# Retention followed by a token-mixing MLP: contiguous q, 128x128 state products, a last batch by chunks, and a new order

## Chip, cores and metric

The kernel runs on one core of a Trainium2 chip. A core has a tensor engine (PE, with its weight loads listed as PEld), a vector engine (DVE), a scalar engine (ACT), GpSimd (POOL), a sync engine (SP) that issues the transfers here, and 16 DMA engines. The metric is the time of one launch in microseconds (us); lower is better.

## The reference

Two blocks follow each other. The first is retention over q, k, v of shape (4 batches, 8 heads, 768 steps, 64), as a recurrence with a decay per head:

```python
gamma = 1.0 - 2.0 ** (-5.0 - np.arange(H))
for t in range(S):
    state = gamma * state + einsum('bhd,bhe->bhde', k[:, :, t], v[:, :, t])
    y[:, :, t] = scale * einsum('bhd,bhde->bhe', q[:, :, t], state)
```

Its output, with the heads side by side, is x of shape (4, 768, 512). The second block mixes tokens within a batch:

```python
W_tok = scale * einsum('bsd,btd->bst', x @ w_q, x @ w_k)
mixed = einsum('bst,btd->bsd', W_tok, x)
out = np.maximum(mixed, 0.0) @ w_out
```

w_q and w_k are 512x64, w_out is 512x512. Inputs and output are float32; the kernel multiplies in bfloat16 and accumulates in float32.

## The kernel before

**Tiles.** A batch has 768 steps: six chunks of 128, taken as three pairs of chunks. There are 12 pairs, numbered 0 to 11, three to a batch; pairs 9 to 11 are the last batch. The eight heads are four head pairs (`HP = 4`), two heads of 64 columns side by side (`x` = 0, 1). In the steps' names the first number is the pair and the second a chunk or a half.

**Retention by chunks.** For a pair the kernel casts k to bfloat16 (`ck`), multiplies v by a decay factor per step and head (`cv`) and casts q (`cq`). PE transposes k and q (`trk`, `trq`), and `ek`, `eq` copy the results from PSUM to SBUF. `sc` multiplies k and q into scores, `eat` applies the causal mask, `ia` multiplies the masked scores with the values, `st` adds the chunk's k and v product to the running state in PSUM bank 7, `es` copies the state to SBUF, and `in` (with `ic` for one type) multiplies q with the carried state. `ex` takes the sum from PSUM, times a decay factor, to x.

**The MLP.** `xt` transposes x on PE, `exT` copies it, `wqk` makes the w_k product (rows are steps) and the w_q product (rows are features), `ew` copies both. The mixing has no mask, so it is factored: `zm` accumulates z, the product of the w_k part and x, over a batch; `ez` copies z; `mx` multiplies z with the w_q part; `r` is the relu; `pj` multiplies by w_out, 4 matmuls of 512 columns to a chunk; `eo` copies the chunk to an output tile; and SP stores it.

**How q lies.** q is loaded with eight steps in a row to a partition, so after the transposes it is in order of (chunk, step, sub-position). `eq` copies it into `qT[128, 2, J*QG, HP]`, and the score matmuls read their moving operand as

```python
return pairs[p]["qT"][rows(x), c, :, hp]
```

that is, with a step of four elements. The products with the carried state read the same slice as their stationary operand.

**Three types of pairs.** `TYPES = "112112111nnn"` says how a pair's k and v are loaded. Types 1 and 2 bring two steps of one head together, runs of 512 bytes; type 1 then splits chunk from chunk in its casts, two instructions on 64 partitions for one chunk, and type 2 keeps the steps interleaved and does its scores and state products in 64x64 tiles. Type n loads one step to a partition, runs of 256 bytes, and casts a chunk in one instruction on 128 partitions.

**Tile forms on PE.** Scores, carried-state products and mixes contract over 64 rows, with the two heads or halves on the two row tiles of the array. State products and z have 64 output rows and use two column tiles. Transposes, values, w products and projections use the whole array.

**Order.** Nothing is scheduled by a compiler. `ORDER` is a list of steps written out by hand; each engine executes its own steps in the order of the list and waits on semaphores. A token `name.pair.part:E@bank` gives the engine (A for ACT, V for DVE, P for GpSimd, none for PE) and the PSUM bank. `fill.15@6` at the start is 15 matmuls on zeros. `LOADS` is the order in which SP issues transfers; a load is issued when one of 16 stage tiles (`STAGES`) is free, that is, when the load 16 places earlier has been cast. The stores (`s0` and so on) stand behind all loads.

Of the kernel before, what the change touches and what calls it, by code (L numbers as in the profile page):

```python
# [16 lines left out]
mask.0:P mask.1:P mask.2:P fill.15@6 ck.0.1:A cv.0.0:P cq.0.1:V cq.0.0:A trq.0@0 ck.1.0:P ck.0.0:V  # L17
eq.0:A cv.0.1:V cv.1.0:P trk.0@6 cv.1.1:P cv.3.1:P st.0.0 cv.3.0:P es.0.0:V ek.0:A sc.0.1@5
eat.0.1:V ck.3.1:P cv.2.1:P sc.0.0@0 in.0.1@2 ck.1.1:A cq.1.0:V trk.1@4 cq.1.1:A eat.0.0:V st.0.1
ek.1:A trq.1@6 eq.1:V sc.1.0@5 cq.2.1:A cq.2.0:V es.0.1:A sc.1.1@0 eat.1.0:V trq.2@4 ia.0.0@2 ck.2:A  # L20
ia.0.1@2 ex.0:V W:P st.1.0 eq.2:A ia.1.0@5 ck.4.1:P cq.4.0:P ck.4.0:P trk.2@4 cv.4.1:P es.1.0:A
st.1.1 in.1.1@5 cv.4.0:P cq.3.0:A eat.1.1:V cq.5:P es.1.1:A in.1.0@5 ek.2:A cq.3.1:V ck.3.0:A WO.0:P
xt.0@2 ia.1.1@5 ck.5.0:P ck.7.0:P trq.3@0 cv.5.0:P ex.1:V ck.6.0:P sc.2.1@3 eq.3:A cq.7:P eat.2.1:V
sc.2.0@5 trk.3@3 xt.1@0 ek.3:A cv.2.0:V st.2.0 eat.2.0:V es.2.0:V ck.6.1:P cv.6.1:P sc.3.1@3
eat.3.1:V in.2@5 exT.0:A exT.1:A ic.2@5 ia.2.0@5 ia.2.1@5 ex.2:V cq.4.1:A sc.3.0@1 st.3.0 es.3.0:A
wqk.0@3 trq.4@0 eat.3.0:V xt.2@6 ew.0:A eq.4:A trk.4@5 ia.3.1@3 in.3.1@3 exT.2:V ia.3.0@3 ex.3:V
cq.6.0:P st.3.1 cv.6.0:P wqk.1@6 ek.4:A wqk.2@5 ew.2:A sc.4.1@2 sc.4.0@0 ew.1:A cv.7.1:P ck.5.1:V
xt.3@4 exT.3:A zm.2@5 es.3.1:V zm.0@5 cq.8.0:P eat.4.1:V zm.1@5 st.4.0 eat.4.0:V ia.4.1@2 ck.8.1:P
trq.5@4 eq.5:V ez.0:A mx.0@5 es.4.0:A in.4.0@2 mx.2@0 in.4.1@2 r.0:A st.4.1 es.4.1:A WO.1:V ia.4.0@2
cq.9:P trk.5@4 ek.5:A wqk.3@6 ew.3:A pj.0.0@5 eo.0.0:A ex.4:V xt.4@2 sc.5.0@3 sc.5.1@5 r.2:A  # L30
cv.8.0:P cv.5.1:V st.5.0 es.5.0:A ck.7.1:A exT.4:V pj.0.1@2 eat.5.0:V eat.5.1:V cv.8.1:P wqk.4@0
ew.4:A ic.5@3 in.5@3 ia.5.0@3 eo.0.1:V ia.5.1@3 ck.9.1:P cv.9.1:P ex.5:V mx.1@0 r.1:A cq.6.1:A
ck.10.0:P trk.7@6 trq.7@2 cv.9.0:P ek.7:V trk.6@5 xt.5@3 exT.5:V pj.1.0@4 eo.1.0:A trq.6@6 eq.6:A
wqk.5@3 ew.5:A ek.6:V cq.10:P pj.2.0@4 eo.2.0:A eq.7:V sc.7.1@5 sc.6.0@1 st.6.0 es.6.0:A zm.3@3
ck.11.0:P zm.5@3 zm.4@3 ez.1:A st.6.1 es.6.1:A cv.7.0:V ck.10.1:P pj.2.1@4 eo.2.1:A st.7.0 eat.6.0:V
sc.7.0@2 eat.7.1:V es.7.0:A mx.5@0 sc.6.1@5 r.5:A pj.1.1@4 eo.1.1:A eat.7.0:V cq.8.1:A eat.6.1:V
cq.11:P ia.7.1@2 ia.7.0@2 st.7.1 in.7.0@2 in.7.1@2 ex.7:V mx.3@0 in.6.1@4 es.7.1:V pj.5.0@6 ia.6.1@4
r.3:A eo.5.0:A ia.6.0@4 trq.8@0 trq.9@6 ex.6:V pj.3.0@1 ck.8.0:A trk.8@5 xt.7@4 eq.8:V cv.10.0:P
eq.9:A ek.8:A eo.3.0:V pj.5.1@6 eo.5.1:A ck.9.0:V mx.4@0 r.4:A exT.7:V cv.10.1:P sc.8.1@2 eat.8.1:V
sc.8.0@4 eat.8.0:V st.8.0 es.8.0:A pj.3.1@6 eo.3.1:A trk.9@0 ek.9:V pj.4.1@2 eo.4.1:A xt.6@4 exT.6:V  # L40
# [27 lines left out]
def kernel(  # L68
# [9 lines left out]
):  # L78

# [49 lines left out]
    z_left = [NP] * B  # L129
# [13 lines left out]
    def load(name, p, half=None, eng=None):  # L143
# [11 lines left out]
        if TYPES[p] == "n":  # L155
            st[name + "_st"] = stage_pool.tile([128, 2, HP, 2, D], FP32, name=name + "_st", tag="st")
            for c in range(2):
# [34 lines left out]
    def load_token(token):  # L192
        if token[0] in "wo":
            load_weights(token)
        else:
            load(token[0], int(token[1:]))
# [8 lines left out]
    def more_loads():  # L205
        while queue:
            token = queue[0]
            if token[0] == "s":
                if not stored(token[1:]):
                    return  # L210
                queue.pop(0)
                continue
            n = len(staged)
            if n >= STAGES and staged[n - STAGES] not in cast:
                return
            staged.append(token)
            load_token(queue.pop(0))
# [15 lines left out]
    make_identity(nc, identity)  # L233

# [208 lines left out]
    def trk(e, b, p):  # L443
        st = pairs[p]
        ps = bank16(b).rearrange("p (hp i n) -> p hp i n", hp=HP, i=2)
        for hp in range(HP):
            for i in range(2):
                src = st["ks"][:, hp, i] if TYPES[p] == "2" else st["ks"][:, i, hp]
                nc.tensor.transpose(ps[:, hp, i], src.rearrange("p x d -> p (x d)"), identity)  # L449
        st["kT_ps"] = bank16(b)  # L450

    def ek(e, b, p):
        st = pairs[p]
        st["kT"] = kq_pool.tile([128, HP, 2, 128], BF16, name="kT")
        copy(e, st["kT"].rearrange("p hp i n -> p (hp i n)"), st["kT_ps"])
# [13 lines left out]
    def trq(e, b, p):  # L469
        st = pairs[p]  # L470
        ps = bank16(b).rearrange("p (c j n) -> p c j n", c=2, j=J)
        for j in range(J):
            nc.tensor.transpose(  # L473
                ps[:, :, j], st["qs"][:, j].rearrange("p x d -> p (x d)"), identity
            )
        st["qT_ps"] = bank16(b)

    def eq(e, b, p):
        st = pairs[p]
        st["qT"] = kq_pool.tile([128, 2, J * QG, HP], BF16, name="qT")  # L480
        copy(e, st["qT"].rearrange("p c t w -> p (c t w)"), st["qT_ps"])

    def qT(p, x, hp, c):
        return pairs[p]["qT"][rows(x), c, :, hp]
# [48 lines left out]
    state_ps = bank32(7)[:, 0 : HP * D].rearrange("p (hp d) -> p hp d", hp=HP)  # L533
# [13 lines left out]
    def inter(e, b, p, c):  # L547
        y = y_of(p, b)
        s_sb = pairs[p]["s", 0] if c == 1 else pairs[p - 1]["s", 1]
        for hp in range(HP):  # L550
            for x in range(2):
# [3 lines left out]
                    rhs=s_sb[rows(x), hp, :],  # L555
# [15 lines left out]
    def inter2(e, b, p):  # L571
        y = y_of2(p, b)
        for hp in range(HP):
            for c in range(2):
                s_sb = carried(p, c)
                if s_sb is None:
# [4 lines left out]
                    rhs=s_sb[rows(c), hp, :],  # L581
# [5 lines left out]
    def cross2(e, b, p):  # L587
        y = y_of2(p, b)
        new = [first(p, 0) if p % NP else False, first(p, 1)]
        for hp in range(HP):  # L590
            for i in range(2):
                for c in range(2):
                    x = 1 - c
                    s_sb = carried(p, c)
                    if s_sb is None:
# [4 lines left out]
                        rhs=s_sb[rows(x), hp, :],  # L600
# [5 lines left out]
    def state1(e, b, p, c):  # L606
        cp = p % NP
        st = pairs[p]
        for hp in range(HP):
            for x in range(2):  # L610
                nc.tensor.matmul(  # L611
                    out=state_ps[rows(x), hp, :],
# [7 lines left out]
    def state2(e, b, p, c):  # L620
        cp = p % NP
        st = pairs[p]
        for hp in range(HP):
            for j in range(2):
                for x in range(2):
                    nc.tensor.matmul(
                        out=state_ps[rows(x), hp, :],
# [7 lines left out]
    def es(e, b, p, c):  # L635
        pairs[p]["s", c] = s_pool.tile([128, HP, D], BF16, name="s_sb")
        copy(e, pairs[p]["s", c], state_ps)

    def ia1(e, b, p, half):
        st = pairs[p]  # L640
        y = y_of(p, b)
        for hi in range(2):
            hp = 2 * half + hi
            for c in range(2):
                for x in range(2):
# [7 lines left out]
                    )  # L653

# [32 lines left out]
    def ex(e, b, p):  # L687
        st = pairs[p]
        st["x"] = x_pool.tile([128, 2, HP, 2, D], BF16, name="x_nat")
        nc.vector.tensor_tensor(  # L690
            out=st["x"].rearrange("p c hp x d -> p x (c hp) d"),
            in0=st["y_ps"].rearrange("p x c hp d -> p x (c hp) d"),
            in1=fy[:, p % NP].rearrange("p x c hp -> p x (c hp)").to_broadcast([128, 2, 2 * HP, D]),
            op=ALU.mult,
        )

    def xt(e, b, p):
        st = pairs[p]
        ps = bank16(b).rearrange("p (a c t) -> p a c t", a=NDM, c=2)
        for c in range(2):  # L700
            for a in range(NDM):
                nc.tensor.transpose(  # L702
                    ps[:, a, c], st["x"][:, c, a].rearrange("p x d -> p (x d)"), identity
                )
        st["xt_ps"] = bank16(b)

    def exT(e, b, p):
        st = pairs[p]
        st["xT"] = xt_pool.tile([128, NDM, 2, C], BF16, name="xT")
        copy(e, st["xT"].rearrange("p a c t -> p (a c t)"), st["xt_ps"])  # L710

    def wqk(e, b, p):
        st = pairs[p]
        wk_ps = bank32(b)[:, 0:128].rearrange("p (h0 c h1) -> p c h0 h1", h0=J, c=2)
        wq_ps = bank32(b)[:, 128:384]
        for c in range(2):
            for a in range(NDM):
                nc.tensor.matmul(  # L718
                    out=wk_ps[:, c, :],
                    lhsT=st["xT"][:, a, c, :],  # L720
                    rhs=wqk_sb[:, a, 2 * DH :],
                    start=(c == 0 and a == 0),
# [166 lines left out]
```

## Time and profile before

| | us |
|---|---|
| Time, median of 3 runs | 103.09 (102.55 to 103.23) |
| Profiled execution, its own time | 102.75 |
| Its span, first to last instruction | 101.0 |
| PE busy | 90.5 |
| DVE busy | 75.4 |
| ACT busy | 63.7 |
| GpSimd busy | 63.2 |
| Bytes moved | 26.69 MB, a mean of 264 GB/s |

The granted clock is TensorE's clock as a share of full speed; its mean over the span is 0.949. A line such as `PE banks L494 x16` in the chain is a run of 16 matmuls at line 494 of the kernel (here a score step); the time beside it is what the chain spent there. A group's line gives busy time and the mean of one instruction in ns, then the idle time ahead of it and what ended it. Matmuls overlap, so the mean of one (288 ns for a score) is far more than its share of the array; the chain's time over a run of them is the cost to use.

### The profile page before, as it was taken

The numbers are of one execution on the slowest core, as the hardware profiler recorded it, in microseconds if no ns is written. First come the engines' busy times: TensorE is split into PE (matmuls) and PEld (weight loads), VectorE is DVE, ScalarE is ACT, GpSimd is POOL, SyncE is SP. The second block draws the span as 40 slices with busy tenths as digits, with TensorE's granted clock in tenths as the row PEclk, the third lists the DMA queues.
The fourth block names the chain that finished last, engine by engine and source line by source line (L and its number), as shares of the span: only waits on it lengthen the run. The fifth ranks groups of instructions, "written<-read, shape, count | busy, mean of one in ns | idle before, by whom it ended". The sixth has DMA issues, their size and how long they took to land.

```text
span 101.0 us, 3421 instructions
## 1 busy us (share of the span) xinstructions
PE 90.5 (90%) x1439; PEld 64.5 (64%) x1439; DVE 75.4 (75%) x107; ACT 63.7 (63%) x101; POOL 63.2 (62%) x87
## 2 busy tenths in 40 slices
PE   5994296996889999999999999999999999999950
PEld 1323186894779889669776776678977777553410
DVE  4217497599996798998899889979687964749510
ACT  4357649488778467975757798664686665623540
POOL 7853999999999998899999999996100000000000
PEclk9999555589999999999999999999999999999999
DMA  0999999998999999999998999999935000522983
GB/s 28 335 276 336 322 353 373 349 305 187 357 341 277 372 352 366 375 380 361 351 243 204 232 299 230 290 292 394 402 116 208 6 0 0 214 108 100 379 313 139
DMA packets 39407, 26.69 MB, mean 264 GB/s; under 512 B 14304, under 2 KB 32736, under 8 KB 39392
## 3 DMA queue, kind: packets, MB, share of 16 engines
q1 hardware_dynamic: 38864, 26.22, 83.6%
q10 hardware_dynamic: 528, 0.26, 0.9%
q8 instruction: 11, 0.18, 0.8%
q14 instruction: 4, 0.03, 0.1%
HBM read 20.19 MB, written 6.29 MB: 262 GB/s over the span
## 4 chain that ended last, share of the span: by engine, by line
PE 71%; DVE 7%; DMA 7%; issue 4%; ACT 3%; POOL 3%; SPq 1%; DVEq 0%; POOLq 0%
PE banks L798 19%; PE banks L494 10%; DMA v_st<-in_v_dram 7%; PE banks L646 5%; PE banks L727 5%; PE banks L449 5%; PE banks L473 5%; PE banks L702 4%; PE banks L611 4%; POOL vs L412 3%; PE banks L718 3%; PE banks L756 3%; PE banks L776 2%; PE banks L552 2%; DVE qT L135 2%
## 5 line engine op out<-in xcount | busy, mean ns | idle before, releaser
L412 POOL TENSOR_TENSOR vs<-v_st,fv 64x512 bf16<-64x512 f32 x24 | 26.4, 1099 | 3.8 <-DMA v_st<-in_v_dram 2.4
L798 PE MATMUL banks<-wout_sb,relu 128*128 128x512 bf16 x96 | 23.9, 380 | 0.0
L526 DVE TENSOR_TENSOR at_sb<-banks,cmask 128x1024 bf16<-128x1024 f32 x18 | 21.5, 1219 | 1.1 <-PE banks L494 0.8
L134 ACT COPY o_st<-banks 128x512 f32<-128x512 f32 x19 | 11.1, 586 | 12.0 <-PE banks L798 11.7
L690 DVE TENSOR_TENSOR x_nat<-banks,fy 128x1024 bf16<-128x1024 f32 x10 | 12.2, 1220 | 4.5 <-PE banks L646 3.1
L798 PEld LDWEIGHTS <-relu 128*128 128x128 bf16 x96 | 8.3, 98 | 8.5 <-issue 0.9
L135 POOL CAST ks<-k_st 64x512 bf16<-64x512 f32 (+1 forms) x21 | 12.9, 621 | 1.0 <-PE banks L449 0.2
L494 PE MATMUL banks<-qT,kT 64*128 64x128 bf16 x160 | 12.0, 288 | 1.2 <-DVE qT L135 0.8
L791 ACT ACTIVATE relu<-banks 128x1024 bf16<-128x1024 f32 x9 | 9.2, 1027 | 2.9 <-PE banks L776 2.9
L134 ACT COPY kT<-banks 128x1024 bf16<-128x1024 bf16 x8 | 8.1, 1014 | 3.5 <-PE banks L449 3.5
L494 PEld LDWEIGHTS <-kT 64*128 64x128 bf16 x160 | 7.9, 107 | 2.8 <-issue 1.9
L611 PE MATMUL banks<-vs,ks 128*64 128x64 bf16 x144 | 5.9, 208 | 3.1 <-POOL vs L412 3.1
L134 ACT CAST ks<-k_st 64x512 bf16<-64x512 f32 (+2 forms) x12 | 7.8, 654 | 1.2 <-DMA k_st<-in_k_dram 1.1
L449 PE MATMUL banks<-identity,ks 128*128 128x128 bf16 x96 | 7.9, 230 | 0.7 <-DVE at_sb L526 0.7
L134 ACT COPY qT<-banks 128x1024 bf16<-128x1024 bf16 x7 | 7.1, 1013 | 2.2 <-PE banks L473 2.2
L473 PE MATMUL banks<-identity,qs 128*128 128x128 bf16 x96 | 8.1, 234 | 0.3 <-ACT qs L134 0.3
L135 POOL CAST qs<-q_st 128x1024 bf16<-128x1024 f32 (+1 forms) x8 | 7.7, 962 | 0.7 <-DMA q_st<-in_q_dram 0.4
L646 PE MATMUL banks<-vs,at_sb 128*128 128x64 bf16 x160 | 8.0, 201 | 0.0
L526 DVE TENSOR_TENSOR at_sb<-banks,cmask_n 128x1024 bf16<-128x1024 f32 x6 | 7.2, 1219 | 0.9 <-PE banks L494 0.7
L134 ACT CAST s_sb<-banks 128x256 bf16<-128x256 f32 x16 | 6.0, 375 | 2.9 <-PE banks L611 1.7
L611 PEld LDWEIGHTS <-ks 128*64 128x64 bf16 x144 | 4.2, 117 | 5.6 <-issue 4.6
L727 PE MATMUL banks<-xT,wqk_w 128*128 128x256 bf16 x48 | 7.2, 273 | 0.3 <-issue 0.3
(80 smaller groups left out, 156.7 us busy)
## 6 DMA issues: line engine op xcount, KB each, us to landing
q_st<-in_q_dram SPq DMA_DIRECT2D x12, 512.0 KB, 6.8
v_st<-in_v_dram SPq DMA_DIRECT2D x9, 512.0 KB, 7.0
out_dram<-o_st SPq DMA_DIRECT2D x9, 512.0 KB, 6.3
k_st<-in_k_dram SPq DMA_DIRECT2D x8, 512.0 KB, 6.9
k_st<-in_k_dram SPq DMA_DIRECT2D x7, 256.0 KB, 4.2
v_st<-in_v_dram SPq DMA_DIRECT2D x6, 256.0 KB, 5.4
out_dram<-o_st SPq DMA_DIRECT2D x6, 256.0 KB, 2.0
o_st<-in_moe_w_out_dram SPq DMA_DIRECT2D x2, 512.0 KB, 6.1
```

What stands on the lines that cost most here:

```text
L134: return nc.scalar.copy(out=out, in_=in_)
L135: return ENGINES[e].tensor_copy(out=out, in_=in_)
L412: ENGINES[e].tensor_tensor(out=st["vs"][rows(j), c].rearrange("p hp x d -> p (hp x) d"), in0=st["v_st"][rows(c), :, :, j].rearrange("p hp ...
L449: nc.tensor.transpose(ps[:, hp, i], src.rearrange("p x d -> p (x d)"), identity)
L473: nc.tensor.transpose(ps[:, :, j], st["qs"][:, j].rearrange("p x d -> p (x d)"), identity)
L494: nc.tensor.matmul(out=ps[:, x, hi, c, :], lhsT=st["kT"][rows(x), hp, c, :], rhs=qT(p, x, hp, c), start=(hi == 0 and c == 0), stop=(hi == ...
L526: ENGINES[e].tensor_tensor(out=st["at", half].rearrange("p x hi i t -> p (x hi i t)").rearrange("p (m n) -> p m n", n=n), in0=st["at_ps", ...
L611: nc.tensor.matmul(out=state_ps[rows(x), hp, :], lhsT=st["ks"][:, c, hp, x, :], rhs=st["vs"][:, c, hp, x, :], start=(cp == 0 and c == 0 an ...
L646: nc.tensor.matmul(out=y[:, x, c, hp, :], lhsT=st["at", half][:, x, hi, c, :], rhs=st["vs"][:, c, hp, x, :], start=first(p, x), stop=False ...
L690: nc.vector.tensor_tensor(out=st["x"].rearrange("p c hp x d -> p x (c hp) d"), in0=st["y_ps"].rearrange("p x c hp d -> p x (c hp) d"), in1 ...
L727: nc.tensor.matmul(out=wq_ps, lhsT=wqk_sb[:, a, 0 : 2 * DH], rhs=st["xT"][:, a].rearrange("p c t -> p (c t)"), start=False, stop=(a == NDM ...
L798: nc.tensor.matmul(out=bank32(b), lhsT=st["relu"][:, a, c, :], rhs=wout_sb[:, a, :], start=(a == 0), stop=(a == NDM - 1),)
```

## The change

- **q.** The transposes of q multiply by `identity_q`, the identity with its columns regrouped, so that a head pair's q comes out contiguous: `qT[128, 2, HP, J*QG]`, read as `[rows(x), c, hp, :]`. Transposes and copies stay the same in number and size.
- **State.** `WIDE_STATE`: a state product is one 128x128 matmul to a head pair (4 to a chunk) instead of two of 64 columns (8 to a chunk); the blocks between different heads are computed and not read. Bank 7 holds 128x512, and `es` copies all of it.
- **Transposes by 64 rows.** For the pairs marked in `HALVED` (6 of 12 for k, 4 for q, 3 for x) a step is 16 transposes of 64 rows each, on the two row tiles and into two banks, instead of 8 of 128 rows.
- **Types.** `"111n11nnnnnn"`: type 2 is gone, pairs 3, 6, 7 and 8 become type n. The mask for type 2 is not built.
- **The last batch by chunks.** For pairs 9, 10 and 11 (`SPLIT`) `ia`, `ex`, `xt`, `exT`, the w products, `ew` and `zm` go by chunks, `mx` by chunks within a step, and `r` by chunks. v of these pairs is loaded by halves, as tokens of their own (`v9a`, `v9b`).
- **Steps.** `wqk` is cut into `wk` and `wq`.
- **Zero matmuls.** Besides the 15 at the start, 24 more stand between the steps of the first pairs (four, five, three and so on).
- **Order.** Both lists, `ORDER` and `LOADS`, are new. Stores still stand behind all loads. `PLAIN_Q` and `TWO_WQ` are options that stay off.

```diff
-mask.0:P mask.1:P mask.2:P fill.15@6 ck.0.1:A cv.0.0:P cq.0.1:V cq.0.0:A trq.0@0 ck.1.0:P ck.0.0:V
...
+mask.0:P mask.2:P fill.15@6 ck.0.1:A ck.0.0:V trk.0@0 cq.0.0:V cq.0.1:P fill.4@6 trq.0@1 eq.0:A
+ek.0:V fill.5@6 sc.0.1@0 sc.0.0@2 ck.1.0:A cv.0.1:V cv.0.0:P fill.3@6 st.0.0 es.0.0:A fill.3@6
...
+cv.11.0:P es.10.1:A in.10.1@3 sc.11.0@5 in.10.0@3 eat.11.0:V ia.10.1@3 ex.10.1:V wk.9.0@0 wq.9.0
+ew.9.0:A st.11.0 es.11.0:A pj.6.0@2 eo.6.0:A mx.8@5 r.8:A in.11.0@0 in.11.1@0 cv.11.1:P ia.11.1@0
+ia.11.0@0 xt.10.1@2 exT.10.1:A ex.10.0:V xt.10.0@3 exT.10.0:A pj.7.1@4 eo.7.1:A ex.11.1:V xt.11.1@5
+ex.11.0:V xt.11.0@0 exT.11.0:V wk.10.1@2 wq.10.1 exT.11.1:V pj.8.1@3 wk.10.0@6 wq.10.0 wk.11.0@5
+wq.11.0 wk.11.1@4 wq.11.1 eo.8.1:V zm.9.1@3 zm.9.0@3 ew.11.0:V zm.11.0@3 ew.10.1:A ew.10.0:A
+zm.10.0@3 zm.10.1@3 ew.11.1:A zm.11.1@3 pj.7.0@4 eo.7.0:A ez.3.0:V mx.11@2 mx.9@5 r.9.0:A mx.10@0
+r.9.1:V pj.8.0@4 r.10.1:A r.10.0:V eo.8.0:V pj.9.1@6 eo.9.1:A pj.9.0@0 eo.9.0:V pj.10.0@6 eo.10.0:A
+pj.10.1@4 eo.10.1:A r.11.0:V pj.11.0@6 eo.11.0:A r.11.1:V pj.11.1@4 eo.11.1:A
...
-q0 v0 k1 v1 q1 q2 k2 v3 q3 k3 v2 w k4 q4 v4 k5 k7 q5 o0 o1 v5 k6 q7 v6 q6 v7 q8 k8 q9 v8 v9 k9 k10
-q10 k11 q11 v10 v11 s0 s2 s1 s5 s3 s4 s6 s7 s8 s11/1 s11/0 s9/0 s9/1 s10/0 s10/1
+q0 v0 k1 q1 v1 k2 v2 q2 w k3 q3 v3 k4 q4 v4 q5 k5 o0 o1 v5 q6 k6 k7 q7 v6 q8 v7 k8 v8 q9 v9a k9 q10
+k10 v9b k11 q11 v10a v10b v11b v11a s0 s1 s2 s3 s4 s5 s6 s7 s8 s9/1 s9/0 s10/0 s10/1 s11/0 s11/1
...
-TYPES = "112112111nnn"
+TYPES = "111n11nnnnnn"
+HALVED = dict(k="000000111111", q="000000100111", x="000000110001")
+SPLIT = (9, 10, 11, )
+WIDE_STATE = 1
...
+    identity_q = const_pool.tile([128, 128], BF16, name="identity_q")
+    for c in range(2):
+        nc.vector.tensor_copy(
+            out=identity_q[:, rows(c)].rearrange("p (w g) -> p w g", w=HP),
+            in_=identity[:, rows(c)].rearrange("p (g w) -> p w g", w=HP),
+        )
...
     def qT(p, x, hp, c):
-        return pairs[p]["qT"][rows(x), c, :, hp]
+        return pairs[p]["qT"][rows(x), c, hp, :]
...
+            if WIDE_STATE:
+                nc.tensor.matmul(
+                    out=state_ps[:, hp].rearrange("p x d -> p (x d)"),
+                    lhsT=st["ks"][:, c, hp].rearrange("p x d -> p (x d)"),
+                    rhs=st["vs"][:, c, hp].rearrange("p x d -> p (x d)"),
...
+                if halved:
+                    for r in range(2):
+                        nc.tensor.transpose(
+                            ps[:, r, hp, i], src[rows(r)], identity[rows(r), rows(r)]
+                        )
...
+    def ia_chunk(e, b, p, c):
+        st = pairs[p]
+        y = y_of(p, b)
+        for hp in range(HP):
+            for x in range(2):
+                nc.tensor.matmul(
+                    out=y[:, x, c, hp, :],
+                    lhsT=st["at", hp // 2][:, x, hp % 2, c, :],
+                    rhs=st["vs"][:, c, hp, x, :],
```

More of the change, by code (lines that the diff above doesn't have):

```diff
@@ L155, in load @@
         if TYPES[p] == "n":
-            st[name + "_st"] = stage_pool.tile([128, 2, HP, 2, D], FP32, name=name + "_st", tag="st")
-            for c in range(2):
+            if name + "_st" not in st:
+                st[name + "_st"] = stage_pool.tile(
+                    [128, 2, HP, 2, D], FP32, name=name + "_st", tag="st"
+                )
+            for c in range(2) if half is None else [half]:
                 (eng or nc.sync).dma_start(
@@ new lines, in ew @@
+    def ew(e, b, p, c=None):
+        st = pairs[p]
+        if c is None:
+            n = 128 + wcols(p)
+            w = moe_pool.tile([128, n], BF16, name=f"wqk_n{n}")
+            copy(
+                e,
+                w.rearrange("p (i g j) -> p i g j", g=QG, j=J),
+                st["w_ps"].rearrange("p (i j g) -> p i g j", g=QG, j=J),
+            )
+            st["wk"] = [w[:, 0:64], w[:, 64:128]]
+            wqT = w[:, 128:].rearrange("p (c t) -> p c t", t=C)
+            st["wqT"] = [wqT[:, i % wqT.shape[1]] for i in range(2)]
+            st["wq_both"] = w[:, 128:]
+        else:
+            if "wk" not in st:
+                st["wk"], st["wqT"] = [None] * 2, [None] * 2
+            w = moe_pool.tile([128, 192], BF16, name="wqk_n192")
+            copy(
+                e,
+                w.rearrange("p (g j) -> p g j", j=J),
+                st["w_ps", c].rearrange("p j g -> p g j"),
+            )
+            st["wk"][c] = w[:, 0:64]
+            st["wqT"][c] = w[:, 64:192]
@@ L772, in mx @@
         z = z_sbs[p // NP]
+        st["mx_ps"] = bank32(b, 2)
+        if TWO_WQ[p // NP] == "1":
+            ps = bank32(b, 2).rearrange("p (c half ai t) -> p c half ai t", c=2, half=2, ai=2)
+            for half in range(2):
+                for ai in range(2):
+                    for c in range(2):
+                        nc.tensor.matmul(
+                            out=ps[:, c, half, ai, :],
+                            lhsT=z[rows(c), half ^ c, ai, :],
+                            rhs=st["wqT"][c][rows(c), :],
+                            start=(half == 0 and ai == 0),
+                            stop=(half == 1 and ai == 1),
+                            skip_group_check=True,
+                        )
+            return
@@ L773, in mx @@
         ps = bank32(b, 2).rearrange("p (half ai t) -> p half ai t", half=2, ai=2)
+        wqTs = st["wqT"] if p in SPLIT else [st["wq_both"]]
+        n = 2 * C // len(wqTs)
         for ai in range(2):
-            for half in range(2):
-                nc.tensor.matmul(
-                    out=ps[:, half, ai, :],
-                    lhsT=z[rows(half), ai, :],
-                    rhs=st["wqT"][rows(half), :],
-                    start=(ai == 0),
-                    stop=(ai == 1),
-                    skip_group_check=True,
-                )
@@ L784, in mx @@
-        st["mx_ps"] = bank32(b, 2)
-    def r(e, b, p):
-        st = pairs[p]
-        st["relu"] = relu_pool.tile([128, NDM, 2, C], BF16, name="relu")
-        dst = st["relu"].rearrange("p a j t -> p (a j t)")
+            for c, wqT in enumerate(wqTs):
+                for half in range(2):
+                    nc.tensor.matmul(
+                        out=ps[:, half, ai, c * n : c * n + n],
+                        lhsT=z[rows(half), 0, ai, :],
+                        rhs=wqT[rows(half), :],
+                        start=(ai == 0 and c == 0),
+                        stop=(ai == 1),
+                        skip_group_check=True,
+                    )
```

344 lines of the change are left out of this document (229 added, 115 removed).

## The prediction, written before the result

> **What bounds the kernel now.** I read the page first: busy shares, the forty slices, the chain.
>
> ```profile
> PE 90.5 (90%) x1439; PEld 64.5 (64%) x1439; DVE 75.4 (75%) x107; ACT 63.7 (63%) x101; POOL 63.2 (62%) x87
> PE   5994296996889999999999999999999999999950
> PEclk9999555589999999999999999999999999999999
> PE 71%; DVE 7%; DMA 7%; issue 4%; ACT 3%; POOL 3%; SPq 1%; DVEq 0%; POOLq 0%
> ```
>
> PE has almost no gap from slice 11 (27 us) to 97.5 us, and the chain lies on it for 71% of the span. Between 10 and 20 us PE has gaps and its granted clock is halved. Then I asked for stretches by window (span, busy time of PE, PEld, DVE, ACT, POOL with instruction counts, then granted clock, DMA share, GB/s), for the end of GpSimd's work, and for the load queue's own waits.
>
> ```profile
> 9.10:12.10 3.00, 0.01 (x2) 0.01 (x2) 2.02 (x2) 2.55 (x4) 2.85 (x2) 0.74 1.04 315
> 12.00:20.40 8.40, 7.53 (x112) 6.58 (x112) 5.99 (x8) 4.65 (x8) 7.83 (x10) 0.50 1.10 362
> 34.00:50.00 16.00, 15.91 (x323) 12.63 (x319) 14.71 (x18) 11.17 (x19) 14.61 (x18) 1.00 1.10 367
> 52.00:64.00 12.00, 11.91 (x196) 8.43 (x194) 11.13 (x13) 9.67 (x16) 11.56 (x13) 1.00 1.02 242
> 55.70:69.90 14.20, 14.11 (x235) 10.11 (x233) 12.81 (x15) 10.23 (x16) 13.22 (x15) 1.00 1.08 283
> 60.00:62.00 2.00, 2.00 (x28) 1.53 (x26) 2.00 (x4) 1.97 (x4) 2.00 (x4) 1.00 1.03 181
> ...
> 69.97 1.04 POOL L433 TENSOR_TENSOR vs<-v_st,fn 128x512 bf16<-128x512 f32 x1 [0.78 <-DMA v_st<-in_v_dram]
> ...
> SPq L150 <- POOL ks L135: 10.0, 5, 3.4
> ```
>
> The DMA engines are full too, from 2 us until the last value lands at 69.97 us, where GpSimd waits for it. In 34-50 us, where k and v come in runs of 512 bytes and q in runs of 2 KB, they move 367 GB/s; in 52-64 us, where most of the traffic is "n" pairs in runs of 256 bytes, 242. So there are two limits: the loads until 70 us, and a backlog of PE work that takes another 27.5 us.
>
> **What PE's steps cost.** From the chain in order of time (start, us, what):
>
> ```profile
> 12.52 1.02 PE banks L494 x16
> 13.76 0.97 PE banks L449 x8
> 32.34 0.25 PE banks L552 x8
> 42.15 1.03 PE banks L512 x25
> 50.25 0.86 PE banks L798 x4
> 55.15 0.46 PE banks L494 x8
> 57.67 0.22 PE banks L776 x4
> 57.89 0.13 PE banks L552 x8
> 70.00 0.23 PE banks L646 x8
> 70.24 0.23 PE banks L718 x8
> 70.47 0.44 PE banks L727 x4
> 71.36 0.45 PE banks L449 x8
> 76.74 0.24 PE banks L611 x8
> 76.98 0.66 PE banks L756 x12
> 77.64 0.12 PE banks L611 x8
> 78.32 0.27 PE banks L552 x16
> 91.13 6.33 PE banks L798 x28
> ```
>
> Eight transposes (L449) take 0.97 us at half clock and 0.45 at full clock. Sixteen score matmuls (L494) take 1.02 at half clock and 2 x 0.46 at full clock: they hardly follow the array's clock, so something that feeds them sets the pace. Their moving operand is q with a step of four elements. The mix matmuls (L776) use the same 64-row tiles with a contiguous moving operand: 1024 columns in 0.22, against 1024 columns in 0.46 for a half of scores. So contiguous q should bring a half of scores to 0.22. Second, the same step costs 0.11 to 0.12 more behind another tile form: L611 is 0.12 behind L756 (both 64-column tiles) and 0.24 behind L494; L552 is 0.13 or 0.25. A change of form costs about 0.11.
>
> **The change on PE, counted over both orders.** Before: 36 transpose steps x 0.45 = 16.2; 20 halves of scores x 0.46 = 9.2; 4 halves of type 2 (16 at 1.03/25) 2.6; 24 state products x 0.12 = 2.9; products with the carried state 3.0; 24 x 0.23 (L646) = 5.5; 12 x (0.23 + 0.44) (L718, L727) = 8.0; L756 and L776 24 x 0.22 = 5.3; 24 projections x 0.86 = 20.6; 67 changes of form x 0.11 = 7.4. Sum 80.7. After: 23 transposes x 0.45 and 13 by 64 rows x 0.27 (sixteen of 64 columns, the shape of L552 x16) = 13.9; 24 halves of scores x 0.22 = 5.3; 24 state products as four matmuls of 128 columns, half of a transpose step, x 0.22 = 5.3; 20 x 0.13 = 2.6; then 5.5, 8.0, 5.3 and 20.6 as before (the split of the last batch keeps the columns), and 74 changes of form 8.1. Sum 74.6, so 6.1 us less. Bounds: if the step of q is not what slows the scores, 24 x 0.24 = 5.8 come back and nothing is saved; if the 64-row transposes don't overlap, 13 x 0.18 = 2.3 come back. A gain beyond 6.1 has no row.
>
> The row of L552 is weighed against a rule here: the Trainium skill (TensorE: Matmul & The Clock Gate, Back-to-back issue gap) has about 25 ns from start to start however few columns there are. By it a 64-row transpose step would be 16 x 25 = 0.40, and PE's sum 1.7 us higher; the row has 0.27 for 16, which is 17 ns, so the trace disagrees.
>
> The 24 extra zero matmuls (512 columns, 0.86/4 = 0.22 each at full clock, 5.2 us; up to twice that at half clock) stand in the first 30 us, where PE waits for data: it was busy for 0.01 of 3.00 us at 9.1. They should keep the granted clock at 1.0 where it was 0.50, but what follows there waits for loads, so I count nothing for either; without that cover they would delay the first pairs by 5 us.
>
> **The other engines.**
>
> ```profile
> L412 POOL TENSOR_TENSOR vs<-v_st,fv 64x512 bf16<-64x512 f32 x24 | 26.4, 1099 | 3.8 <-DMA v_st<-in_v_dram 2.4
> L433 POOL TENSOR_TENSOR vs<-v_st,fn 128x512 bf16<-128x512 f32 x6 | 6.2, 1042 | 0.8 <-DMA v_st<-in_v_dram 0.8
> L134 ACT CAST s_sb<-banks 128x256 bf16<-128x256 f32 x16 | 6.0, 375 | 2.9 <-PE banks L611 1.7 <-PE banks L626 0.5 <-ACT qs L134 0.4
> L134 ACT COPY o_st<-banks 128x512 f32<-128x512 f32 x19 | 11.1, 586 | 12.0 <-PE banks L798 11.7
> ```
>
> An "n" chunk of values is one instruction of 1.04 instead of two of 1.10; with the steps that move to GpSimd its sum falls from 63 to about 59. The state copy doubles to 128x512; 19 on ACT at 0.586 (that shape, from the output row; at least the old 0.375) make 11.1 instead of 6.0, so ACT goes from 64 to about 68. DVE keeps its 24 mask multiplies and lands near 73. At 0.92 busy (14.71 of 16 us in 34-50) this fits in 80 us, so none of them should be the limit: their cover is that PE now has gaps.
>
> **What ends it: the loads, then a tail.** Pairs 3, 6, 7 and 8 change from 512- to 256-byte runs, 1.049 MB of k and v each: 2.86 us a pair at 367. In 52-64, 12 x 242 = 2.90 MB came; two q loads (1.05 MB, 2.86 us) taken off, 1.85 MB in 9.14 us is 203 GB/s, or 5.2 us a pair. In 55.7-69.9, 4.02 MB less the same q is 2.97 MB in 11.34 us, 262 GB/s, 4.0 us. The extra is 1.1 to 2.3 us a pair; the row of 181 gives 2.9, and all of 283 gives 0.85. I take 1.4, nearer the lower one, since 52-64 also holds waits of the load queue: 4 x 1.4 = 5.6. The last value lands at 75.6 (bounds 73.4 to 81.7).
>
> Its first user is the multiply of chunk 0 of pair 11 (the second half lands first): 1.04, so 76.6. Chunk 1 is multiplied behind it, while PE has other work. From there the order leaves PE: the last state product 0.22, one projection 0.86, mix 0.33, carried state 0.26, values 0.57, two chunk transposes 0.45, projection 0.86, 64-row transposes 0.48, four chunks of L718/L727 1.34, projection 0.86, six chunks of L756 0.88, projection 0.86, three mixes 0.77, seven projections 6.13 (with the form changes): 14.9. About 1.0 of waiting (the last chunk's w copy ahead of L756) makes 15.9, so the last matmul ends at 92.5. Behind it stays what is there now: 101.0 - 97.46 (91.13 + 6.33) = 3.54, one eviction and one 256 KB store. Span 96.0. The profiled run took 102.75 with its span of 101.0, so 1.75 lie around it: 97.8. That run lies 0.34 below the median of 103.09, inside the spread of the three (102.55 to 103.23), and I add nothing for that.
>
> **The rivals.** (B) Short packets are nearly free: landing at 73.4, all else as above, 95.6, and near 93.5 if the tail's waits vanish and the first loads lose their gaps. For it: part of 52-64 was queue waits. Against it: 181 in 60-62 with a DMA share of 1.03. (C) The scores don't gain: PE holds 80.4 us of work again and stays the limit; what remains is the half clock of 12-20.4 (7.53 busy, at most 3.8 back), and 0.5 to 3.8 less gives 99 to 102; I take 101. Against it: L494 at two clocks. (D) DVE becomes the limit by waiting in order: 73 us from 7.2 us on, at a busy share of 0.83 in place of 0.92, ends at 95.2, plus one projection and the 3.54: span 99.6, 101.3. For it: PE no longer has a backlog that hides small waits. (E) The other side: the load queue. Its issues stand in order behind free stage tiles; it waited 10.0 us for GpSimd's k casts (3.4 at longest) and the transfers already issued covered that. If the casts come later, because ACT carries 5 us more and the order deals them out differently, a wait that outlasts the backlog delays every later load one for one. 6.5 us of this puts the landing at 82.1 and the time at 104.3; it decides from a landing of 81.2. Against it: GpSimd's sum falls.
>
> **How the numbers follow.** Forecast 0.44, B 0.20, C 0.09, D 0.12, E 0.15. The time is 97.8. The forecast alone spans 95.5 to 100.5 by the landing; down to 93.0 takes in B, up to 102.8 C and D; what is left out is E and the far ends. About 1% (1.03 us) is what a measurement here can tell from no change. Faster by over 1% (below 102.06): forecast 0.43, B 0.20, C 0.06, D 0.07, so 0.76. Within 1%: 0.01 + 0.03 + 0.04 + 0.01 = 0.09. Slower: 0.15.
>
> **What would show it.** Right: sixteen scores in about 0.45 in the chain; the granted clock near 1.0 from 10 to 20; the last v landing at 74 to 78; PE with gaps before that and about 15 us of PE work behind it; state copies near 0.59. Wrong: scores still at 0.9 (C); the last v before 73.5 (B) or after 81 (E); PE as full as now from 27 us on; or PE waiting mostly for DVE in the middle (D).

## The result, and the profile after

The changed kernel takes 98.93 us (98.71 to 99.15) against 102.82 (101.39 to 103.23 in four runs): a ratio of 0.967, 95% interval 0.963 to 0.971. The ratio leaves out launches in a slower state, into which some of the kernel before fall, so it is not 98.93 over 102.82. The forecast was 97.8, in a range of 93.0 to 102.8. The profiled execution took 98.88 with a span of 97.2.

The page of the changed kernel, its parts 1, 2 and 4:

```profile
PE 86.6 (89%) x1415; PEld 57.4 (59%) x1415; DVE 72.7 (75%) x108; ACT 66.3 (68%) x103; POOL 60.1 (62%) x83
PE   4999696979799998999999999979789999998950
PEclk9999999999999999999999999999999999999999
PE 55%; POOL 16%; DMA 11%; ACT 6%; issue 4%; DVE 2%; SPq 1%; POOLq 0%; ACTq 0%
```

The granted clock no longer dips. PE's part of the chain falls from 71% to 55%; GpSimd now has 16% and the DMAs 11%. The stretches by window (span, busy time of PE, PEld, DVE, ACT, POOL, then clock, DMA share, GB/s):

```profile
20.00:30.00 10.00, 8.47 (x153) 6.42 (x150) 8.42 (x10) 7.84 (x11) 8.96 (x13) 1.00 1.04 305
45.00:75.00 30.00, 28.41 (x621) 20.59 (x620) 23.95 (x28) 22.80 (x36) 20.11 (x25) 1.00 1.00 241
62.80:70.90 8.10, 6.54 (x142) 4.74 (x141) 6.66 (x8) 5.46 (x8) 4.44 (x6) 1.00 1.07 259
```

The timeline of GpSimd, its last multiply of values:

```profile
76.24 2.04 POOL L461 TENSOR_TENSOR vs<-v_st,fn 128x512 bf16<-128x512 f32 x2 [1.56 <-DMA v_st<-in_v_dram]
```

The last value lands at 76.24 instead of 69.97, with 241 GB/s in the middle of the run. Between 62.8 and 70.9 us PE is busy for 6.54 of 8.10 us: there it waits for loads. From the chain in order of time:

```profile
24.88 0.39 PE banks L850 x8
...
37.73 0.63 PE banks L727 x16
38.35 0.34 PE banks L623 x16
38.69 0.22 PE banks L559 x8
38.91 0.33 PE banks L682 x4
...
44.40 0.22 PE banks L682 x4
...
45.40 0.23 PE banks L484 x16
...
63.79 4.29 DMA k_st<-in_k_dram
...
70.26 0.62 POOL ks L147
...
70.93 0.38 PE banks L484 x14
...
86.64 0.98 PE banks L1000 x4
...
87.70 0.60 ACT relu L993
...
88.33 0.70 DVE relu L995
...
89.08 4.49 PE banks L1000 x20
```

L559 is the score step (a half in 0.22), L682 the wide state product (0.22, or 0.33 behind another tile form), L484 a transpose of k by 64 rows (0.23), L1000 the projection. PE is on the chain without a break from 37.73 to 62.79. What PE itself waits for behind that is in its timeline (in brackets the idle time just before, and what ended it):

```profile
65.04 0.41 PE L534 MATMUL banks<-identity_q,qs 64*128 64x64 bf16 x16 [0.50 <-POOL qs L147]
...
70.93 0.38 PE L484 MATMUL banks<-identity,ks 64*128 64x64 bf16 x14 [1.09 <-POOL ks L147]
...
87.88 1.04 PE L1000 MATMUL banks<-wout_sb,relu 128*128 128x512 bf16 x4 [0.28 <-DVE relu L995]
89.08 4.48 PE L1000 MATMUL banks<-wout_sb,relu 128*128 128x512 bf16 x20 [0.16 <-DVE relu L995]
```

It waits 0.50 us for a q and 1.09 us for the last k (cast at 70.26). From 87.62 to 89.08 the chain lies on two relus, one behind the other; PE runs another projection in that time (87.88) and stands for only 0.28 and 0.16 us. Its last matmul ends at 93.57, against 97.46 before.

### The profile page after: what moved, and what is told of

Its sections match the earlier page's. It is cut to its first block, busy times and chain, and to the rows that moved or that the text cites. A ratio compares the mean times of both kernels' runs of the same rounds, so it can differ in the third digit from the quotient of the medians.

```text
span 97.2 us, 3381 instructions
## 1 busy us (share of the span) xinstructions
PE 86.6 (89%) x1415; PEld 57.4 (59%) x1415; DVE 72.7 (75%) x108; ACT 66.3 (68%) x103; POOL 60.1 (62%) x83
## 4 chain that ended last, share of the span: by engine, by line
PE 55%; POOL 16%; DMA 11%; ACT 6%; issue 4%; DVE 2%; SPq 1%; POOLq 0%; ACTq 0%
PE banks L1000 19%; POOL vs L440 9%; DMA v_st<-in_v_dram 7%; POOL ks L147 4%; DMA k_st<-in_k_dram 4%; PE banks L727 4%; PE banks L559 3%; PE banks L682 3%; PE banks L926 3%; PE banks L972 3%; PE banks L874 3%; PE banks L818 3%; PE banks L623 3%; PE banks L850 3%; PE banks L536 2%
## 5 line engine op out<-in xcount | busy, mean ns | idle before, releaser
L1000 PE MATMUL banks<-wout_sb,relu 128*128 128x512 bf16 x96 | 23.8, 379 | 0.4 <-DVE relu L995 0.4
L440 POOL TENSOR_TENSOR vs<-v_st,fv 64x512 bf16<-64x512 f32 x16 | 18.4, 1149 | 3.1 <-DMA v_st<-in_v_dram 2.2
L591 DVE TENSOR_TENSOR at_sb<-banks,cmask_n 128x1024 bf16<-128x1024 f32 x14 | 16.8, 1221 | 2.2 <-PE banks L559 1.3
L461 POOL TENSOR_TENSOR vs<-v_st,fn 128x512 bf16<-128x512 f32 x14 | 14.3, 1042 | 4.0 <-DMA v_st<-in_v_dram 3.9
L147 POOL CAST ks<-k_st 128x512 bf16<-128x512 f32 (+1 forms) x21 | 13.0, 631 | 3.3 <-DMA k_st<-in_k_dram 2.8
L1000 PEld LDWEIGHTS <-relu 128*128 128x128 bf16 x96 | 8.4, 98 | 9.2 <-issue 1.1
L387 PE MATMUL banks<-warm 128*128 128x512 bf16 x39 | 11.6, 438 | 2.1 <-DVE warm L248 1.2
L146 ACT CAST s_sb<-banks 128x512 bf16<-128x512 f32 x19 | 11.1, 587 | 3.2 <-PE banks L682 2.9
L591 DVE TENSOR_TENSOR at_sb<-banks,cmask 128x1024 bf16<-128x1024 f32 x10 | 11.9, 1218 | 1.1 <-PE banks L559 1.1
L993 ACT ACTIVATE relu<-banks 128x1024 bf16<-128x1024 f32 (+1 forms) x11 | 10.3, 946 | 2.1 <-PE banks L972 1.2
L147 POOL CAST qs<-q_st 128x512 bf16<-128x512 f32 (+1 forms) x10 | 7.6, 764 | 6.6 <-DMA q_st<-in_q_dram 6.4
L682 PE MATMUL banks<-vs,ks 128*128 128x128 bf16 x80 | 7.8, 220 | 1.6 <-POOL vs L440 1.5
L559 PE MATMUL banks<-qT,kT 64*128 64x128 bf16 x192 | 8.8, 217 | 0.0
L682 PEld LDWEIGHTS <-ks 128*128 128x128 bf16 x80 | 5.1, 98 | 3.9 <-issue 2.2
L559 PEld LDWEIGHTS <-kT 64*128 64x128 bf16 x192 | 5.8, 94 | 2.8 <-issue 1.9
```

The costliest lines, as they stand in the source:

```text
L146: return nc.scalar.copy(out=out, in_=in_)
L147: return ENGINES[e].tensor_copy(out=out, in_=in_)
L387: nc.tensor.matmul(out=bank32(b), lhsT=warm[:, 0:128], rhs=warm, start=True, stop=True)
L440: ENGINES[e].tensor_tensor(out=st["vs"][rows(j), c].rearrange("p hp x d -> p (hp x) d"), in0=st["v_st"][rows(c), :, :, j].rearrange("p hp ...
L461: ENGINES[e].tensor_tensor(out=st["vs"][:, c].rearrange("p hp x d -> p (hp x) d"), in0=st["v_st"][:, c].rearrange("p hp x d -> p (hp x) d" ...
L559: nc.tensor.matmul(out=ps[:, x, hi, c, :], lhsT=st["kT"][rows(x), hp, c, :], rhs=qT(p, x, hp, c), start=(hi == 0 and c == 0), stop=(hi == ...
```

## The experiments

Ratios are to the kernel before, measured on the same chip, with 95% intervals; a point is 1% of its time, 1.03 us. The changed kernel itself has 0.967 (0.963 to 0.971).

**Contiguous q alone, in the old order.**

```diff
 kernel before
-        ps = bank16(b).rearrange("p (c j n) -> p c j n", c=2, j=J)
+        ps = bank16(b).rearrange("p (c w j g) -> p (c w) j g", c=2, w=HP, j=J)
...
-                ps[:, :, j], st["qs"][:, j].rearrange("p x d -> p (x d)"), identity
+                ps[:, :, j], st["qs"][:, j].rearrange("p x d -> p (x d)"), identity_q
...
-        return pairs[p]["qT"][rows(x), c, :, hp]
+        return pairs[p]["qT"][rows(x), c, hp, :]
```

> The kernel before with contiguous q as its only change (the regrouped identity and the new layout of qT; old order, old types, old loads). Theory 1 (q's step of four set the pace of the scores, and PE's backlog sets the end of the old kernel): sixteen scores fall from 0.92 to 0.45 us in the chain, PE loses 20 x 0.24 + 4 halves of type 2 at 0.2 to 0.3 each = 5.6 to 6.0 us, all of it behind 27 us where PE has no gaps, so 102.8 falls to 97 to 99. Theory 2 (the scores are paced by the row tiles or by their weight loads, not by q's step): scores stay at 0.9, 102 to 103. Theory 3 (the scores get faster, but the old order then waits for DVE at 0.92 busy): scores at 0.45, 100 to 102.

Measured: 0.971 (0.962 to 0.979). On its page the granted clock still dips; in its chain, in order of time, sixteen scores (L501) take 0.45 us and a half 0.22:

```profile
PEclk9999655579999999999999999999999999999998
```

```profile
46.63 0.62 POOL qs L135
...
60.77 0.45 PE banks L501 x16
...
65.00 0.22 PE banks L501 x8
...
86.35 6.34 PE banks L805 x28
```

Theory 1 stands on the cause: q's step set the pace of the scores. PE's busy time falls by 5.8 us (90.5 to 84.7); by the ratio about 3.0 us of that reach the end, 99.8 in place of 102.8, between the ranges of theories 1 and 3. The chain shows what is in the way: GpSimd's casts, and not DVE as theory 3 had it, are on it up to 47 us, and only then PE takes over. One edit gives what the whole change gives, within the intervals.

**Strided q put back into the changed kernel.**

```diff
-                    nc.tensor.transpose(ps[:, c, :, j], src[rows(c)], identity_q[rows(c), rows(c)])
+                    nc.tensor.transpose(ps[:, c, j], src[rows(c)], identity[rows(c), rows(c)])
...
-        return pairs[p]["qT"][rows(x), c, hp, :]
+        return pairs[p]["qT"][rows(x), c, :, hp]
```

> The changed kernel with q strided again (plain identity, old layout of qT), all else kept. Theory 1 (the loads set the end, PE has a gap of 1.6 us only between 60 and 80 us and none from 40 to 60): 24 x 0.24 = 5.8 us come back on PE, of which its gaps before 76 us take some 2 to 3, so 98.9 rises to 101.5 to 103. Rival (PE is well hidden behind the loads): at most 1 us, 99 to 100.

Measured: 0.993 (0.989 to 0.997), 2.6 points or 2.7 us slower than the changed kernel. In its chain a half of scores is back at the old price:

```profile
39.70 0.46 PE banks L559 x8
```

PE's busy time rises by 5.0 us (86.6 to 91.6), where 5.8 were expected, and its last matmul ends 2.8 us later (96.40 against 93.57), so PE's idle time up to there falls by 2.2. That is theory 1: about a half comes through, and PE's gaps take the rest.

**Long runs in the changed kernel.**

```diff
-                    out=st[name + "_st"][:, c].rearrange("t hp x d -> t (hp x) d"),
-                    in_=src[b, :, t0 + c * C : t0 + (c + 1) * C, :].rearrange("h t d -> t h d"),
+                    out=st[name + "_st"][:, c].rearrange("t hp x d -> t hp (x d)"),
+                    in_=src[b, HP * c : HP * c + HP, t0 : t0 + 2 * C, :].rearrange(
+                        "h (g j) d -> g h (j d)", j=2
+                    ),
```

> The changed kernel with k and v of the seven n pairs loaded in runs of 512 bytes into the same tiles: same bytes, same number of transfers, same casts. The tiles then hold the values of other heads and steps, so the values are not those of the reference; times are. Theory 1 (packets of 256 bytes cost 1.4 to 2 us a pair and the late loads hold PE up): GB/s in 45 to 75 us rises from 241 to 330 or more, the last v lands 6 to 10 us earlier than 76.2, PE's wait for the last k (1.1 us at 69.8) goes, and the time falls to 96 to 98, no further since PE has no other gaps. Theory 2 (the loads alone set the end, and the tail of 17 us follows them): 90 to 93. Theory 3 (short packets are nearly free): no change, 98.5 to 99.3.

Measured: 0.957 (0.952 to 0.962), 1.0 point better. First a window of the changed kernel, then those of this run, and below them its last values in GpSimd's timeline:

```profile
45.00:60.00 15.00, 15.00 (x318) 10.71 (x318) 12.71 (x14) 11.77 (x19) 10.38 (x13) 1.00 0.97 236
```

```profile
45.00:60.00 15.00, 15.00 (x318) 10.61 (x315) 12.71 (x15) 11.67 (x20) 15.00 (x20) 1.00 1.08 341
60.00:70.00 10.00, 10.00 (x230) 7.12 (x228) 8.06 (x9) 8.02 (x12) 5.83 (x7) 1.00 1.08 384
70.00:80.00 10.00, 9.96 (x196) 7.30 (x194) 9.03 (x13) 8.86 (x15) 0.00 (x0) 1.00 0.18 66
```

```profile
65.72 2.04 POOL L463 TENSOR_TENSOR vs<-v_st,fn 128x512 bf16<-128x512 f32 x2 [1.28 <-DMA v_st<-in_v_dram]
```

The last value lands 10.5 us earlier and the time falls by about 1 us. PE is simply full: 15.00 of 15.00, 10.00 of 10.00 and 9.96 of 10.00. So the short packets do cost the loads 10.5 us, and the loads hardly set the end: theory 2 and theory 3 fall. In 45 to 60 us the loads move 341 GB/s in place of 236. This bears out the Trainium skill (DMA: Bandwidth & Descriptors, Specifications), which puts the full rate at transfers of 512 bytes and up.

**No zero matmuls behind the first 15.** All `fill` steps but the first are taken out of `ORDER`.

> The changed kernel without the 24 zero matmuls behind the first 15. Theory 1 (the first 30 us wait for loads and GpSimd, whatever the clock): the granted clock falls to about 0.5 somewhere between 8 and 20 us, and the time stays within 0.7 us of 98.9, either way. Rival A (the cold clock delays the first pairs and this is never made up, since PE is full from 37 to 63 us): 100 to 102. Rival B (the zero matmuls stand in the way of work): 97 to 98.3.

Measured: 0.965 (0.957 to 0.973), no difference that can be told. The clock falls as expected:

```profile
PEclk9999955599999999999999999999999999999999
```

The chain lies on loads and GpSimd's casts up to 25 us at either clock, and PE comes on it at nearly the same place, 25.77 here and 24.88 in the changed kernel. Of these 0.9 us 0.6 are there when the first v lands, at 9.02 against 8.44:

```profile
25.77 0.39 PE banks L850 x8
```

**Narrow state products.** `WIDE_STATE = 0`.

> The changed kernel with state products of two 64-column tiles again (8 matmuls, state copies of 128x256). Theory 1 (a change of tile form costs 0.11 us): 24 x (0.12 - 0.22) = -2.4 us on PE, 95 changes of form instead of 74 = +2.3, so PE is unchanged; ACT loses 19 x 0.21 = 4.0 us, which is off the path; 98.4 to 99.4. Rival A (the wide product is what saves, by fewer matmuls): 100 or more. Rival B (the doubled state copies on ACT delay the products with the carried state): 97 to 98.

Measured: 0.968 (0.958 to 0.979), no difference that can be told. PE's busy time is 86.0 against 86.6 us, which fits theory 1: what the wide product costs PE in columns it saves in changes of form. ACT's busy time falls from 66.3 to 62.7 us, off the path.

**Full transposes.** `HALVED` all zeros.

> The changed kernel with all transposes as 8 matmuls of 128 rows. Theory 1 (a 64-row transpose step takes 0.23 where a full one takes 0.45, and PE is full from 37 to 63 and from 71 us): 13 x 0.22 = 2.9 us more on PE, with 73 changes of form instead of 74; the gaps of 1.6 us between 60 and 80 take part of it, so 1.0 to 2.5 us more, 100 to 101.4. Rival (hidden behind the loads of the last batch, since 10 of the 13 steps belong to pairs 6 to 11): within 0.5 us of 98.9.

Measured: 0.984 (0.976 to 0.991), 1.7 points slower. Transposes by 64 rows pay. That is theory 1: of an expected 2.9 us on PE some 1.7 reach the end.

**Four relu buffers.** `relu_pool = pool("relu", 4)`.

> The changed kernel with four buffers for the relu instead of two. In its tail ACT and DVE take the relus one after the other (ACT 87.70 for 0.60, then DVE 88.33 for 0.69, PE waiting). Theory 1 (the first half of a relu waits for the projection that read its buffer two pairs earlier, and the other engine's half waits behind it): with more buffers both halves start with the mix, the chain loses 1.0 to 1.4 us at its end, 97.5 to 98.0. Rival (two engines that read one mix result from the same banks, or write one tile, are put one behind the other whatever the buffers): no change, 98.5 to 99.3.

Measured: 0.971 (0.963 to 0.978), no difference that can be told. From the timelines of ACT and DVE:

```profile
85.52 1.09 ACT L993 ACTIVATE relu<-banks 128x512 bf16<-128x512 f32 x2
86.15 1.29 DVE L995 TENSOR_SCALAR relu<-banks 128x512 bf16<-128x512 f32 x2 [1.73 <-ACT relu L993]
```

For pair 9 the rival holds: DVE's half still starts where ACT's ends, so two engines' halves of one mix go one after the other, whatever the buffers. Whether the shared banks or the shared tile put them in order stays open. For pair 10 theory 1 holds: ACT takes its half directly behind the first, where in the changed kernel it waited 0.60 us (until 87.70) for a projection. In PE's timeline the last 28 matmuls take 6.6 us instead of 7.0. The 1.0 to 1.4 us that theory 1 hoped for were never there to win: PE stood for only 0.44 us between the relus.

**n pairs early.** `TYPES = "1nnn11n11nnn"`.

> The changed kernel with types 1nnn11n11nnn: pairs 1 and 2 become n, pairs 7 and 8 become 1, so the bytes in short runs stay the same. Theory 1 (GpSimd's casts are the path of the first 25 us, 16% of the chain, and GpSimd has slack after 45 us): its casts there fall by 3 x 1.16 for v and 2 x 0.64 for k = 4.8 us, PE's first full stretch starts 2 to 4 us earlier, PE is then the limit, and the time falls by 1 to 3 us to 96 to 98. Rival A (the first pairs wait for loads, which get 1.8 us a pair slower in short runs): 98.5 to 101. Rival B (casts of type 1 on GpSimd at 50 to 60 us delay the late loads or PE): over 99.5.

Measured: 1.009 (1.003 to 1.016), 4.2 points slower than the changed kernel. Theory 1 falls, and what both rivals name is seen. Two windows of the changed kernel, the same two of this run, and one piece of its chain:

```profile
7.00:20.00 13.00, 11.14 (x164) 7.42 (x161) 11.51 (x11) 8.77 (x14) 10.86 (x11) 1.00 1.08 308
50.00:65.00 15.00, 14.54 (x298) 9.98 (x294) 12.39 (x14) 11.82 (x18) 9.66 (x12) 1.00 0.95 223
```

```profile
7.00:20.00 13.00, 11.08 (x165) 7.63 (x163) 9.58 (x9) 6.79 (x10) 7.79 (x8) 1.00 1.05 256
50.00:65.00 15.00, 12.10 (x244) 8.93 (x244) 11.11 (x13) 9.62 (x14) 14.19 (x17) 1.00 1.04 279
```

```profile
26.62 6.69 DMA v_st<-in_v_dram
```

GpSimd had less to do before 20 us but waited for data, which came at 256 GB/s instead of 308; a v load came into the chain at 26.6; and from 50 to 65 GpSimd was nearly full (14.19 of 15.00) with the longer casts of pairs 7 and 8 while PE had gaps (12.10 busy instead of 14.54). How the 4.2 points divide between the two is not shown; the sum lies outside rival A's range.

**The changed kernel again, and three attempts to beat it,** on one chip:

```diff
 tail and k11
-... trk.11@2 ek.11:A zm.6@4 zm.7@4 zm.8@4 ez.2.0:A ia.9.0@5 ex.9.0:V st.9.1 es.9.1:A xt.9.1@2 ...
+... zm.6@4 zm.7@4 zm.8@4 ez.2.0:A ia.9.0@5 ex.9.0:V st.9.1 es.9.1:A trk.11@2 ek.11:A xt.9.1@2 ...
-r.9.0:A mx.10@0 r.9.1:V pj.8.0@4 r.10.1:A r.10.0:V
+r.9.1:A mx.10@0 r.9.0:A pj.8.0@4 r.10.1:V r.10.0:V
-    relu_pool = pool("relu", 2)
+    relu_pool = pool("relu", 4)
 also w on ACT:                W:P -> W:A
 also pair 8 in long runs:     TYPES = "111n11nn1nnn"
```

> The changed kernel itself, beside the three below on the same chip, so that they can be compared with it. All theories: a ratio of 0.96 to 0.975 to the kernel before.

> The changed kernel with three edits: four relu buffers; both halves of pair 9's relu on ACT and both of pair 10's on DVE; and the transposes of pair 11's k (with their copy) moved behind the z products of pairs 6 to 8, the values of chunk 0 of pair 9 and a state product, 1.3 us of PE work that does not need the late k. Theory 1 (two halves of one mix on two engines go one after the other, and PE waits 1.1 us for the last k with work behind it): PE's wait before the last projections falls from 1.4 to 0.6 us or less, its wait for k from 1.1 to near 0, and 1.0 to 2.0 us go: 0.983 to 0.99 of the changed kernel. Rival (what is saved at one wait is lost at the next, since the last v lands at 76 us whatever PE does): within 0.5 us of the changed kernel.

> The kernel e10 with the cast of w_q and w_k on ACT instead of GpSimd (1.7 us of GpSimd's work at 23 us, the last piece of its path before PE's first full stretch). Theory 1 (GpSimd's casts are the path of the first 25 us, and PE is the limit from 37 us on): 0.4 to 1.2 us less than e10. Rival (the loads are the path there, as they were when pairs 1 and 2 came in short runs): within 0.3 us of e10, or more where ACT is late.

> The kernel e10 with pair 8 of type 1 (k and v in runs of 512 bytes; GpSimd casts it in halves, 3.6 us more). Theory 1 (short runs cost 1.4 to 2 us a pair, and GpSimd has slack after 50 us): the last v lands 1 to 2 us earlier, and with PE's wait for the loads nearly gone the time falls by 0 to 0.6 us against e10. Rival (GpSimd's longer casts of pair 8 hold up the casts of pairs 9 and 10 behind them in its order, as with pairs 7 and 8): 0.5 to 2 us more than e10.

Measured: the changed kernel 0.967 (0.961 to 0.973); with the tail and k11 edits 0.971 (0.965 to 0.976); with w on ACT 0.988 (0.979 to 0.997); with pair 8 in long runs 0.983 (0.975 to 0.991). None beats the changed kernel. The chain of the second:

```profile
72.05 1.03 ACT kT L146
...
73.12 0.38 PE banks L818 x4
...
86.49 0.78 PE banks L972 x24
87.27 6.31 PE banks L1000 x28
```

and in PE's timeline:

```profile
73.12 0.38 PE L818 MATMUL banks<-identity,x_nat 128*128 128x128 bf16 x4 [1.25 <-ACT kT L146]
```

The two relu edits do what was hoped: the last 28 matmuls of the projections run in one piece of 6.31 us. The moved transposes win nothing: they use bank 2, the next transposes of x use it too, and PE now stands for 1.25 us, until ACT has copied k out of it at 73.12, where it stood 1.09 us for the late k. The projections begin 0.6 us later (87.27 against 86.64), and the last matmul ends at 93.58, as in the first profile of the changed kernel (93.57). Halves of one mix on one engine were not run alone. On ACT the w cast came into the chain at 26.2 us, behind a copy of k, where GpSimd had finished it at 24.84 in the first profile of the changed kernel and at 25.39 with the tail and k11 edits alone; this was the rival's second case. PE's step that needs it starts at 27.32 instead of 25.43, and the last matmul ends at 94.93 instead of 93.58. With pair 8 of type 1, GpSimd's casts came into the chain from 54 to 65 us, and the last value landed at 77.20, not earlier.

## Why the prediction was right, and where it was not

**The terms on PE.** Half of scores 0.22 forecast, 0.22 measured, and the cause (q's step) is shown from both sides, by adding it alone and by taking it away. A change of tile form 0.11: L682 is 0.22 or 0.33. Wide state 0.22, and worth nothing that could be measured. The count was off there: both orders hold 20 state products, not 24 (the last chunk of a batch needs none), so the wide ones cost PE 2.0 us more and not 2.4, and the sums should have differed by 6.5 us and not 6.1. Transposes by 64 rows: 0.27 forecast, 0.23 measured. At 14 ns from start to start this lies further below the floor of about 25 ns in the Trainium skill (TensorE: Matmul & The Clock Gate, Back-to-back issue gap) than the 17 ns of before. But the sixteen alternate between two row tiles, and each tile starts one in 29 ns: the floor may hold for one tile by itself, and no run here tells.

**Zero matmuls worth nothing.** Right, as far as leaving them out can tell (0.965 against 0.967).

**The price of short runs.** 1.4 us a pair was forecast for four pairs, and a landing at 75.6; it came at 76.24. Long runs for all seven n pairs bring it to 65.72, or 1.5 us a pair (10.5 / 7): right.

**Which limit ends it: this step failed.** I let the loads set the end and added a tail of 15.9 us. The tail is nearly the right length (77.2 to 93.57 is 16.4), so the numbers came out. But with the last value 10.5 us earlier the time falls by only 1 us: PE's own work reached pair 11 at about the time when its values came, and the two limits happen to lie together. PE never waits for the last value: the state product that uses it starts at 77.66, 0.4 us after its multiply ends. That the forecast comes within 1.1 us is in this respect luck. One of the prediction's signs of being wrong, PE as full as now from 27 us on, nearly came: from there PE stands for 2.5 us, against 0.5 before. What sets the time is PE, full from 37.7 us on, with waits of 0.50, 1.09 and 0.44 us.

**GpSimd as no limit: failed too.** I covered the other engines with the gaps that PE would have. Late in the run that holds, but in the first 25 us GpSimd's casts, fed by the loads, are the chain (14.6 of the 15.8 us that GpSimd has on it), and PE's full stretch comes behind them: where the cast of w came later, on ACT, PE's next step starts 1.9 us later (27.32 against 25.43) and the last matmul ends 1.35 us later. That this part is fixed by loads and casts together, and not by GpSimd's sum, is what the run with n pairs early showed: less casting there, later data, slower.

**Where the gain on PE went.** PE's last matmul ends 3.9 us earlier (97.46 to 93.57). From 27 us on to that end, first before and then after:

```profile
27.00:97.47 70.47, 69.97 (x1176) 50.31 (x1176) 57.74 (x63) 46.41 (x75) 40.80 (x48) 1.00 0.83 257
```

```profile
27.00:93.58 66.58, 64.05 (x1133) 43.01 (x1129) 52.62 (x63) 48.59 (x77) 38.25 (x46) 1.00 0.95 274
```

PE's work falls by 5.9 us, and its idle time grows by 2.0, from 0.50 to 2.53: that is the 3.9. Of the 2.53 about 0.5 lie before 37.7 us, 1.59 are the waits for q and k, and 0.44 those between the relus. The 5.9 need not be the forecast sum, since the two orders have not done the same work by 27 us. The forecast had 1.0 of waiting in the tail, at another place. The wait at the relus is shown to be removable, and is worth 0.6 us (the last 28 matmuls take 6.93 us from 86.64 to 93.57, and 6.31 in one piece); it was not gained on its own. The last batch by chunks, the new order and the new types were not tried by themselves.

**The rivals.** B (short runs nearly free) falls by the run with long runs. C (scores don't gain) falls. D (DVE takes over) falls: 23.95 of 30 us in 45-75. E, the load queue, did not decide in the changed kernel: the landing at 76.24 is well short of 81.2, though the queue (SPq) has 7% of the chain in the second profile of that kernel. With pairs 1 and 2 of type n it has 25%, all of it before the v load at 26.62, and the kernel is slower than the one before (1.009). Whether late k casts held it there, as E has it, is not shown.

## What to carry to other kernels

Give TensorE's moving operand a contiguous last dimension: here it halved the cost of the scores, and that one edit was worth the whole rewrite, within the intervals. When a sum of terms meets the time, still move each limit by itself: the landing of the loads could be brought 10 us forward for 1 us. A piece of the chain is not idle time of the engine behind it: the relus had 1.46 us of the chain and cost PE 0.6. Before moving a step to fill a wait, look at who uses its PSUM bank next. Two halves of one result on two engines went one after the other here; on one engine, with four buffers, PE did not wait for them.

## What the runs showed of the hardware that I had not expected

A moving operand with a step of four bfloat16 elements took 0.46 us for 1024 columns on two row tiles and 0.22 when contiguous, and in the strided form nearly the same at half the granted clock (1.02 for sixteen matmuls against 0.92). Sixteen 64-row transposes take 0.23 us, the eight 128-row ones that they replace 0.45. In the changed kernel a granted clock of about 0.5 in slices 6 to 8 cost nothing that could be measured; its chain lies there on loads and GpSimd at either clock.
